# An attention scan with two gated layers on one core: the last two A parts in unit 13, the last substitution at 1.05 steps a part, weight conversions cut into single operations in units 18 to 23

## The chip, the cores and the metric

The kernel runs on one core of one Trainium2 chip. The metric is the device time of one execution in microseconds; the median of three runs of the kernel before is 929.41 us (926.57 to 936.09). The two halves of the kernel share one program: first the attention, whose last third holds the change, then two layers.

## The reference

Inputs are r, k, v, w, a, b of shape 4 x 8 x 768 x 40 (batch, head, step, head dim) in float32, and the weights of two layers. The layers' matrices w_in, w_out, w_in2, w_out2 and the taps are float64 and reach the chip as 64-bit words. The reference is, cut to its core:

```
for t in range(S):                       # S = 768, state: B x H x 40 x 40
    y[t]  = r[t] @ state
    Sa    = state @ a[t]
    state = state*w[t][None,:] - outer(Sa, b[t]) + outer(v[t], k[t])
x = y as (4, 768, 320)
h = relu(x @ w_in);  c = 3-tap convolution of h over steps
x = (h * sigmoid(c)) @ w_out
h = relu(x @ w_in2); u, v = halves of h
x = (u * (w_spatial @ normalized(v) + b_spatial)) @ w_out2
```

## The kernel before

**Units.** The scan is cut into 6 blocks of 128 steps (n = 0 to 5), each of two chunks of 64, for 4 batches (i = 0 to 3) with all 8 heads. A pair (i, n) is a unit; the 24 units are numbered kk = 4n + i. Two batches share a pair of tiles, so a block has two parts p = 2n + i//2. The state passes from unit kk to kk+4.

**The work of a unit** is written as four generators, each yielding after a few instructions. A(kk) (line 148) transposes AR and P on PE, lets ACT copy them to bdA (L159) and PT (L168), and multiplies them (L174); DVE masks the product into G (L175). The last A of a block sends a slice of G to DRAM (tb, L181, four DMAs). Bp(kk) (L231) applies the inverse triangular blocks DT and D1: pf, px, and pw, which ACT copies to WT (L296); POOL copies DT into bdN (L278). Cp(kk) (L317) is the step over the two chunks: pu on PE, its copy to ZU on ACT (L329), pm on PE, and on DVE pm and VM (L339, L341), from which the next chunk's pu is made. Units of the last block have no pm in their second chunk. Dp(kk) (L343) makes the output: pz and pv, ACT's copies ZV and bdR, pS, DVE's SS (L376), py and DVE's y (L387).

**The order.** In the main loop (line 483) each unit kk runs through a written string of 19 positions, `ORDER="CDCBDDCBDACAABBAADD"`. C steps Cp(kk), D steps Dp(kk-1), B steps Bp(kk+1), and A steps A(kk+LA) with LA = 9, nine units ahead. Unit 0 has two A parts, 8 and 9, interleaved in it, two steps at each letter A. Engines take their instructions in the order in which this loop emits them, and so do the DMA queues of SP. Each unit's own D part ends in the next unit. From unit 15 on there is no A part left, and the string's letters A do nothing.

**Ticks.** Every position is a tick. `later(m,f)` runs f after m ticks, in the order of the list. At every tick `pump` advances the background generators: `acc` grows by RATE0, RATE or RATE2 (1.25), and as many steps run as acc holds whole ones.

**Substitution** (subst, L185). When the fourth A part of a block has been emitted, subst(n) is started: LL ticks after (LL2 = 9 for the last) it loads L from tb (L189), SUB = 5 ticks after that it joins the background. For each j from 1 to 30 it does a product and a sum on DVE over (31-j) x j elements (L206, L208), one per step; then a copy LT (L211); DDL = 8 ticks after it, `put` stores LT and L to DRAM (dt, dd; L213, L214), and loadD (L219) loads them again as DT (L226) and D1 (L229), as soon as put has run and the B part before has been emitted. These are needed by the B parts of the block. L has one buffer.

**Weights.** Layer weights are converted from 64-bit words to float32 and split into a rounded part and its remainder, during the attention, by one generator (prep1, L618), 14 jobs after the taps: six of 128x512 (w_in), three of 128x320, four of 128x512 (two 256-wide blocks), one of eight 64-wide blocks. A job loads raw by SP (L595), one job ahead; ACT takes its absolute value into mo (L554), DVE does four operations (L555 to L558), and one step later ACT rounds (L606) and POOL subtracts (L607). In the attention the staging tiles use the buffers of tiles that are done with: raw those of AR (two), ct those of PT (two), mo that of bdA (one). The list EX gives the number of steps of this generator that are done by the end of units 14 to 23; within a unit they are spread evenly over the 19 positions. What is left runs with the last D part.

The loop's core, from line 485 on:

```
ahead=[... EARLY[kk] if kk<len(EARLY) else [kk+LA] if kk+LA<NK-2 or not LAST2
       else [NK-2,NK-1] if kk+LA==NK-2 else []]
...
for _ in range(max(1,len(ahead)) if g=='A' else 1): next(gens[g],None)
while done<ex(kk-1)+(ex(kk)-ex(kk-1))*(z+1)//19: next(later_layer,None); done+=1
tick(); acc+=RATE0 if kk<3 else RATE if kk<14 else RATE2; pump(int(acc)); acc-=int(acc)
```

Of the kernel before, what the change touches and what calls it, by code (L numbers as in the profile page):

```python
# [11 lines left out]
def attention(tc, keep, ident, vr,bk,w,a, x, spare=None):  # L12
    nc=tc.nc
# [3 lines left out]
    with ExitStack() as ctx:  # L17
# [69 lines left out]
        def later(m,f):  # L87
            due.append((now[0]+m,f)); 
        def tick():
            now[0]+=1  # L90
            for d in [d for d in due if d[0]<=now[0]]:
                due.remove(d); d[1]()
# [92 lines left out]
        def subst(n):  # L185
            if n not in Ls: Ls[n]=(sb.tile([128,HB*HB+HB],F32,name="L"),sb.tile([128,HB*HB//4],F32,name="tmp"),sb.tile([128,HB,HB],F32,name="LT"))
            flat,tmp,LT=Ls[n]
            L=flat[:,0:HB*HB].rearrange("p (t j) -> p t j",j=HB)
            BQ[0].dma_start(out=L,in_=tb_d[n])  # L189
            yield  # L190
            if n in SMALL:
                K=HB//2
                V.memset(L[:,K:,0:K],0.0)
                Q=flat.rearrange("p (s r) -> p s r",s=2)[:,:,0:K*HB].rearrange("p s (t j) -> p s t j",j=HB)[:,:,:,0:K]
                for j in range(1,K-1):
                    m=K-1-j
                    t=tmp[:,0:2*m*j].rearrange("p (s m k) -> p s m k",s=2,m=m)
                    V.tensor_tensor(t,Q[:,:,j+1:,j:j+1].to_broadcast([128,2,m,j]),Q[:,:,j:j+1,0:j].to_broadcast([128,2,m,j]),ALU.mult)
                    yield
                    V.tensor_tensor(Q[:,:,j+1:,0:j],Q[:,:,j+1:,0:j],t,ALU.add)  # L200
                    yield
            else:
                for j in range(1,HB-1):
                    m=HB-1-j
                    t=tmp[:,0:m*j].rearrange("p (m k) -> p m k",m=m)
                    V.tensor_tensor(t,L[:,j+1:HB,j:j+1].to_broadcast([128,m,j]),L[:,j:j+1,0:j].to_broadcast([128,m,j]),ALU.mult)  # L206
                    yield
                    V.tensor_tensor(L[:,j+1:HB,0:j],L[:,j+1:HB,0:j],t,ALU.add)  # L208
                    yield
            V.memset(flat[:,0:HB*HB:HB+1],1.0)  # L210
            V.tensor_copy(LT,L.rearrange("p t j -> p j t"))  # L211
            def put():
                BQ[0].dma_start(out=dt_d[n],in_=LT)  # L213
                BQ[0].dma_start(out=dd_d[n],in_=L if n in SMALL else L[0:128:2])  # L214
                stored.update((n,j) for j in range(2))
            later(DDL,put)
            yield
        inv={}; stored=set()
        def loadD(p):  # L219
# [175 lines left out]
        def pump(m):  # L395
            while m>0 and (bg or bg2):
                q=bg or bg2
                try: next(q[0])
                except StopIteration: q.pop(0); continue
                m-=1  # L400
# [10 lines left out]
        with tc.manual_schedule(engines={mybir.EngineType.SP,mybir.EngineType.DVE,mybir.EngineType.Activation}):  # L411
# [61 lines left out]
            with tc.manual_schedule():  # L473
                none=iter(()); acc=0.0; dg={}
                def staging(z):
                    def tmp():
                        mo=sb.tile([128,2,512],F32,name="mo",tag="bdA",bufs=1)
                        return [sb.tile([128,512],I32,name="ct",tag="PT",bufs=2),mo[:,0],mo[:,1]]
                    return (lambda: sb.tile([128,512,2],I32,name="raw",tag="AR",bufs=2)),tmp
                later_layer=spare(FC=512,staging=staging) if spare else none  # L480
                done=0
                ex=lambda kk: EX[kk-14] if kk>=14 else 0
                for kk in range(NK):
                    i,n=units[kk]
                    ahead=[z for z in (EARLY[kk] if kk<len(EARLY) else [kk+LA] if kk+LA<NK-2 or not LAST2 else [NK-2,NK-1] if kk+LA==NK-2 else []) if z<NK]
                    gens={'A':chain(*[A(z) for z in ahead]),'B':Bp(kk+1) if kk+1<NK else none,'C':Cp(kk),'D':dg.pop(kk-1) if kk else none}
                    gens['Z']=dg[kk]=Dp(kk)
                    if kk==6 or kk==14: lam_end(n+1)
                    po=(kk+LA)//2 if (kk+LA+1)%2 else (kk+LA+1)//2
                    z=-1  # L490
                    for g in ORDER if kk<TAIL else ORDER2:
                        if g=='W':
                            warm(ident,WM)
                            continue
                        z+=1
                        for _ in range(max(1,len(ahead)) if g=='A' else 1): next(gens[g],None)
                        if z in BX and kk+1<NK and units[kk+1][1] in SMALL: next(gens['B'],None)
                        while done<ex(kk-1)+(ex(kk)-ex(kk-1))*(z+1)//19:
                            next(later_layer,None); done+=1
                        tick(); acc+=RATE0 if kk<3 else RATE if kk<14 else RATE2; pump(int(acc)); acc-=int(acc)  # L500
                        for s,f in SCHED[(kk+LA+1)%2]+SCHEDC[kk%2]:
                            if s==z:
                                if f=='il' and kk==0: later(9,lambda po=po: l_il(po))
                                elif f=='dup' and kk==0: later(11,lambda po=po: l_dup(po))
                                elif f=='pm' and kk==1: later(4,lambda po=po: l_pm(po,V))
                                elif f=='Z' and kk==0: later(24-z,lambda kk=kk: loadZ(kk//2+1))
                                elif f=='Z': loadZ(kk//2+1)
                                elif f=='V': loadV(kk//2+1)
                                else: {'araw':l_araw,'ln':l_ln,'P':l_P,'g':l_g,'ar':l_ar,'il':l_il,'pm':(lambda p: l_pm(p,V)) if PMV else l_pm,'dup':l_dup}[f](po)
                    if any(z%4==3 for z in ahead): nxt=subst(ahead[-1]//4 if ahead[-1]%4==3 else ahead[0]//4); ll=LL if kk+LA<NK-2 else LL2; later(ll,lambda z=nxt: next(z)); later(ll+SUB,lambda z=nxt: bg.append(z))  # L510
                pump(1000)
                for _ in dg.pop(NK-1): next(later_layer,None)
                flush()

TAIL=24
LAST2=0
PUA=1
WM=2
ORDER2="DCCDDBCBACDADDABBAA"
# [1 line left out]
LA=9  # L521
L4T=14
RATE=1.25
RATE2=1.25
RATE0=1.4
SCHED=[[[1, "il"], [11, "araw"], [12, "ln"], [14, "g"], [15, "dup"], [16, "P"], [17, "ar"]], [[3, "pm"]]]
SCHEDC=[[[6, "Z"]], [[10, "V"]]]
SUB=5
TBL=3
LL2=9  # L530
LL=10
DDL=8
DTL=7
# [6 lines left out]
BX=(0,9)  # L540
DTLS=2
W=[34,9,9,12,12,9,8,8,10,10,6]
EX=[3, 7, 7, 9, 11, 15, 20, 24, 28, 30]

# [1 line left out]

def from_f64(nc,out,raw,tmp):

    t,m=tmp
    lw,up=raw[...,0],raw[...,1]
    V=nc.vector
    nc.scalar.activation(m,up.bitcast(F32),AF.Abs)  # L554
    V.tensor_scalar(out=t,in0=up,scalar1=3,scalar2=0x3fffffff,op0=ALU.logical_shift_left,op1=ALU.bitwise_and)  # L555
    V.scalar_tensor_tensor(out=t,in0=lw,scalar=29,in1=t,op0=ALU.logical_shift_right,op1=ALU.bitwise_or)
    V.scalar_tensor_tensor(out=t,in0=up,scalar=-0x40000000,in1=t,op0=ALU.bitwise_and,op1=ALU.bitwise_or)
    V.scalar_tensor_tensor(out=out,in0=m,scalar=TINY,in1=t.bitcast(F32),op0=ALU.is_ge,op1=ALU.mult)  # L558

def words(ap):  # L560
# [3 lines left out]
class Layers:  # L564
# [12 lines left out]
        return (lambda: L.vv([128,256,2],I32,z%3)), (lambda: [L.vv([128,256],d,3+z%2*3+q) for q,d in enumerate((I32,F32,F32))])  # L577


    def weight(L,w,places,FC=256,staging=None,low=None):  # L580


        nc=L.tc.nc; staging=staging or L.staging
        K,F=w.shape; n=-(-K//128); g=max(1,FC//F); fc=min(F,FC)
        jobs=[(k,min(g,n-k),f0) for k in range(0,n,g) for f0 in range(0,F,fc)]
        jobs=[(k,m,f0,min(fc,F-f0)) for k,m,f0 in jobs]
        stg={}
        def load(z):
            k0,m,f0,fc=jobs[z]
            raw,tmp=staging(z)  # L590
            raw=raw(); stg[z]=raw,tmp
            for q in range(m):
                k=k0+q; rows=min(128,K-k*128)
                for j in range(128//rows):
                    nc.sync.dma_start(out=raw[j*rows:(j+1)*rows,q*fc:(q+1)*fc],in_=words(w[k*128:k*128+rows,f0:f0+fc]))  # L595
        load(0)
        for z,(k0,m,f0,fc) in enumerate(jobs):
            if z+1<len(jobs): load(z+1)
            yield
            fs=slice(f0,f0+fc); raw,tmp=stg.pop(z)  # L600
            t,a,o=[x[:,:m*fc] for x in tmp()]
            from_f64(nc,o,raw[:,:m*fc],(t,a))
            yield
            for q in range(m):
                h,l=places(k0+q); oq=o[:,q*fc:(q+1)*fc]
                nc.scalar.copy(h[:,fs],oq)  # L606
                (low or nc.gpsimd).tensor_tensor(l[:,fs],oq,h[:,fs].bitcast(F32),ALU.subtract)  # L607
                if K%128 and k0+q==n-1: nc.gpsimd.memset(l[64:128,fs].bitcast(F32),0.0)
# [467 lines left out]
```

## Time and profile before

| | |
|---|---|
| median of 3 runs | 929.41 us (926.57 to 936.09) |
| profiled execution | 931.44 us, span 929.7 us |
| granted TensorE clock, mean | 0.946 |
| PE busy | 851.0 us, 92% |
| PEld busy | 792.9 us, 85% |
| DVE busy | 650.9 us, 70% |
| ACT busy | 524.3 us, 56% |
| POOL busy | 225.4 us, 24% |

PE is TensorE's matmuls, PEld its weight loads, DVE VectorE, ACT ScalarE, POOL GpSimd, SP SyncE, which issues the DMAs. A row of the timeline has the start (us from the span's start), the duration, the engine, the line of the kernel, the operation, output and input tile, the count of instructions merged into the row, and in brackets the idle time of the engine before it with what ended it. A row of groups has the summed busy time, the mean duration in ns, and the idle time before. A granted clock of 1.00 stands for 2.4 GHz and 0.50 for 1.2 GHz; a window's figure is the mean over it. Matmul ends are modelled.

### The profile page before, as it was taken

How to read it: one execution, taken by the hardware profiler on the slowest of the kernel's cores; microseconds unless marked ns; L12 is line 12 of the kernel's file. 1: busy time of each engine (PE TensorE's matmuls, PEld its weight loads, DVE VectorE, ACT ScalarE, POOL GpSimd, SP SyncE). 2: the span in 40 equal slices, each digit the busy share in tenths (PEclk: the TensorE clock that was granted, in tenths of full speed). 3: DMA queues.
4: the chain of work that ended last, by engine and by line, in shares of the span. 5: the costliest groups of instructions: out<-in, count | busy, mean ns of one | idle time of the engine just before them, and what ended most of it. 6: DMA issues, size and time to landing. Idle time of an engine off the chain costs nothing. (4 is left out here: it accounts for less than half of the span.)

```text
span 929.7 us, 23445 instructions
## 1 busy us (share of the span) xinstructions
PE 851.0 (92%) x9575; PEld 792.9 (85%) x9575; DVE 650.9 (70%) x1472; ACT 524.3 (56%) x1157; POOL 225.4 (24%) x308
## 2 busy tenths in 40 slices
PE   0888689999999999899988889999999999999997
PEld 0577579999989898788976779999999999999997
DVE  6877795596794878976569978357674667656673
ACT  0463575777767766668655655267433764267421
POOL 2110110222221313224310011245221541235221
PEclk9975697999999999989789899999999999999999
DMA  8989894745648436235221330110021001110011
GB/s 215 218 199 211 155 214 92 162 111 134 141 99 195 85 90 171 68 110 152 81 81 56 98 100 8 47 48 1 1 86 40 23 1 47 55 43 1 1 32 57
DMA packets 149189, 86.70 MB, mean 93 GB/s; under 512 B 124176, under 2 KB 138256, under 8 KB 147152
## 3 DMA queue, kind: packets, MB, share of 16 engines
q1 hardware_dynamic: 148800, 84.78, 37.4%
q8 instruction: 77, 1.26, 0.6%
q14 instruction: 40, 0.33, 0.1%
q10 hardware_dynamic: 272, 0.33, 0.1%
HBM read 61.24 MB, written 23.86 MB: 92 GB/s over the span
## 5 line engine op out<-in xcount | busy, mean ns | idle before, releaser
L697 PE MATMUL psp<-spt,vv 128*128 128x384 f32 x576 | 105.5, 338 | 0.5 <-DVE vv L825 0.3
L697 PE MATMUL ph<-XT,G 128*128 128x386 f32 x512 | 101.5, 344 | 0.7 <-DVE XT L730 0.7
L697 PEld LDWEIGHTS psp<-spt,vv 128*128 128x128 f32 x576 | 100.2, 188 | 2.1 <-ACT vv L822 1.0
L697 PEld LDWEIGHTS ph<-XT,G 128*128 128x128 f32 x512 | 92.6, 191 | 1.1 <-DVE XT L730 1.0
L759 POOL TENSOR_TENSOR gl<-c,gh 128x384 fp32r<-128x384 f32 x48 | 66.2, 1379 | 72.1 <-ACT gh L757 57.6
L773 PE MATMUL acc<-gh,G 128*128 128x384 f32 x320 | 68.6, 343 | 9.4 <-ACT gh L757 7.0
L331 POOL COPY ZU<-ZU 64x320 f32<-64x320 f32 x48 | 26.2, 546 | 193.2 <-ACT ZU L329 187.3
L755 DVE TENSOR_TENSOR c<-h,c 128x384 f32<-128x384 f32 x64 | 39.9, 623 | 44.0 <-ACT c L752 43.8
L773 PEld LDWEIGHTS acc<-gh,G 128*128 128x128 f32 x320 | 56.8, 191 | 13.9 <-ACT gh L757 9.7
L174 PE MATMUL p<-PT,bdA 80*128 80x128 f32 x384 | 57.1, 311 | 6.1 <-ACT PT L168 6.1
L208 DVE TENSOR_TENSOR L<-L,tmp 128x30 f32<-128x30 f32 (+9 forms) x150 | 58.7, 391 | 4.1
L174 PEld LDWEIGHTS p<-PT,bdA 80*128 80x128 f32 x384 | 53.4, 223 | 9.3 <-ACT PT L168 9.2
L206 DVE TENSOR_TENSOR tmp<-L 128x30 f32<-128x30 f32 (+9 forms) x150 | 52.6, 350 | 9.7 <-DMA L<-tb 5.9
L375 PE MATMUL pS<-bdR,ZV 80*128 80x128 f32 x384 | 57.1, 294 | 2.0 <-DVE ZV L369 1.5
L846 ACT CAST zh<-u 128x384 fp32r<-128x384 f32 x28 | 14.4, 514 | 73.6 <-DVE u L843 73.6
L847 POOL TENSOR_TENSOR zl<-u,zh 128x384 fp32r<-128x384 f32 x28 | 31.6, 1128 | 98.6 <-ACT zh L846 87.3
L329 ACT COPY ZU<-pu 64x160 f32<-64x160 f32 x96 | 27.5, 286 | 49.6 <-PE pu L327 47.8
L375 PEld LDWEIGHTS pS<-bdR,ZV 80*128 80x128 f32 x384 | 49.3, 201 | 3.7 <-DVE ZV L369 1.7
L295 PE MATMUL pw<-bdN,G 128*104 128x128 f32 x384 | 50.7, 290 | 0.9 <-issue 0.9
L175 DVE TENSOR_TENSOR G<-p,mT 128x512 f32<-128x512 f32 x48 | 32.8, 688 | 25.2 <-PE p L174 24.8
L757 ACT CAST gh<-c 128x384 fp32r<-128x384 f32 x64 | 32.9, 514 | 30.8 <-DVE c L755 28.3
L842 DVE TENSOR_TENSOR psp<-psp,bb 128x384 f32<-128x384 f32 x32 | 18.1, 566 | 45.4 <-PE psp L697 45.2
(186 smaller groups left out, 2118.3 us busy)
## 6 DMA issues: line engine op xcount, KB each, us to landing
P<-in_bk_dram SPq DMA_DIRECT2D x12, 640.0 KB, 5.1
ZU<-in_vr_dram SPq DMA_DIRECT2D x12, 640.0 KB, 7.3
lq<-in_w_dram SPq DMA_DIRECT2D x12, 320.0 KB, 6.8
araw<-in_a_dram SPq DMA_DIRECT2D x12, 320.0 KB, 6.3
lam<-lq SPq DMA_DIRECT2D x12, 320.0 KB, 4.4
lnA<-lam SPq DMA_DIRECT2D x12, 320.0 KB, 7.0
ilam<-lq SPq DMA_DIRECT2D x12, 320.0 KB, 5.5
il<-ilam SPq DMA_DIRECT2D x24, 160.0 KB, 4.3
```

Of the source, the lines that this page charges most:

```text
L174: T.matmul(p3[:,j],lhsT=bdA[:,g*4+j].rearrange("p c t -> p (c t)"),rhs=PTs[g][:,j],start=True,stop=True)
L175: V.tensor_tensor(G[:,hs,0:2*C],p3,mT.rearrange("p a t -> p (a t)").unsqueeze(1).to_broadcast([128,4,2*C]),ALU.mult)
L206: V.tensor_tensor(t,L[:,j+1:HB,j:j+1].to_broadcast([128,m,j]),L[:,j:j+1,0:j].to_broadcast([128,m,j]),ALU.mult)
L208: V.tensor_tensor(L[:,j+1:HB,0:j],L[:,j+1:HB,0:j],t,ALU.add)
L295: T.matmul(p[:104,j],lhsT=G[:,h0+g*4+j,C:],rhs=N[:,g*4+j],start=True,stop=True)
L375: T.matmul(p[:,j].rearrange("p c t -> p (c t)"),lhsT=ZV[:,j,0:2*C],rhs=bdR[:,j].rearrange("p c t -> p (c t)"),start=True,stop=True)
L697: L.tc.nc.tensor.matmul(out,lhsT=l,rhs=r,start=start and i==0,stop=stop and i==len(prs)-1)
L755: V.tensor_tensor(c,h[:,1:TH+1],c,ALU.mult)
L757: AC.copy(gh,c)
L759: def low(v): v.tensor_tensor(gl,c,gh.bitcast(F32),ALU.subtract)
L773: nc.tensor.matmul(acc[m],lhsT=l,rhs=r,start=f==0 and z<5 and z in (0,1,3),stop=f==NF-1 and z>=5)
L847: nc.gpsimd.tensor_tensor(gl,u,gh.bitcast(F32),ALU.subtract)
```

## The change

The last two A parts, 22 and 23, run together in unit 13, two steps at each letter A, as parts 8 and 9 do in unit 0; unit 14 has none. The last substitution is started from unit 13: its load 17 ticks after that unit, its background steps 5 later. RATE2 is 1.05 steps a tick, and it holds from unit 15 on. The last block's put comes 4 ticks after its LT, not 8. A conversion job's four DVE operations are steps of their own, with one empty step behind them, so a job has six steps and not two; the new list EX puts them in units 18 to 23, after the taps in unit 14. mo uses the buffer of bdA and that of il in turn.

```diff
--- before.py
+++ after.py
@@ -213,7 +213,7 @@
                 BQ[0].dma_start(out=dt_d[n],in_=LT)
                 BQ[0].dma_start(out=dd_d[n],in_=L if n in SMALL else L[0:128:2])
                 stored.update((n,j) for j in range(2))
-            later(DDL,put)
+            later(DDL if n<NU-1 else 4,put)
             yield
         inv={}; stored=set()
         def loadD(p):
@@ -474,10 +474,10 @@
                 none=iter(()); acc=0.0; dg={}
                 def staging(z):
                     def tmp():
-                        mo=sb.tile([128,2,512],F32,name="mo",tag="bdA",bufs=1)
+                        mo=sb.tile([128,2,512],F32,name="mo",tag=("bdA","il")[z%2],bufs=1)
                         return [sb.tile([128,512],I32,name="ct",tag="PT",bufs=2),mo[:,0],mo[:,1]]
                     return (lambda: sb.tile([128,512,2],I32,name="raw",tag="AR",bufs=2)),tmp
-                later_layer=spare(FC=512,staging=staging) if spare else none
+                later_layer=spare(FC=512,staging=staging,fine=True) if spare else none
                 done=0
                 ex=lambda kk: EX[kk-14] if kk>=14 else 0
                 for kk in range(NK):
@@ -497,7 +497,7 @@
                         if z in BX and kk+1<NK and units[kk+1][1] in SMALL: next(gens['B'],None)
                         while done<ex(kk-1)+(ex(kk)-ex(kk-1))*(z+1)//19:
                             next(later_layer,None); done+=1
-                        tick(); acc+=RATE0 if kk<3 else RATE if kk<14 else RATE2; pump(int(acc)); acc-=int(acc)
+                        tick(); acc+=RATE0 if kk<3 else RATE if kk<15 else RATE2; pump(int(acc)); acc-=int(acc)
                         for s,f in SCHED[(kk+LA+1)%2]+SCHEDC[kk%2]:
                             if s==z:
                                 if f=='il' and kk==0: later(9,lambda po=po: l_il(po))
@@ -513,7 +513,7 @@
                 flush()
 
 TAIL=24
-LAST2=0
+LAST2=1
 PUA=1
 WM=2
 ORDER2="DCCDDBCBACDADDABBAA"
@@ -521,13 +521,13 @@
 LA=9
 L4T=14
 RATE=1.25
-RATE2=1.25
+RATE2=1.05
 RATE0=1.4
 SCHED=[[[1, "il"], [11, "araw"], [12, "ln"], [14, "g"], [15, "dup"], [16, "P"], [17, "ar"]], [[3, "pm"]]]
 SCHEDC=[[[6, "Z"]], [[10, "V"]]]
 SUB=5
 TBL=3
-LL2=9
+LL2=17
 LL=10
 DDL=8
 DTL=7
@@ -540,21 +540,28 @@
 BX=(0,9)
 DTLS=2
 W=[34,9,9,12,12,9,8,8,10,10,6]
-EX=[3, 7, 7, 9, 11, 15, 20, 24, 28, 30]
+EX=[3, 3, 3, 3, 17, 31, 46, 60, 80, 88]
 
 
 
 TINY=3.4332275390625e-05
 
 def from_f64(nc,out,raw,tmp):
+
+    for _ in f64_steps(nc,out,raw,tmp): pass
+
+def f64_steps(nc,out,raw,tmp):
 
     t,m=tmp
     lw,up=raw[...,0],raw[...,1]
     V=nc.vector
     nc.scalar.activation(m,up.bitcast(F32),AF.Abs)
     V.tensor_scalar(out=t,in0=up,scalar1=3,scalar2=0x3fffffff,op0=ALU.logical_shift_left,op1=ALU.bitwise_and)
+    yield
     V.scalar_tensor_tensor(out=t,in0=lw,scalar=29,in1=t,op0=ALU.logical_shift_right,op1=ALU.bitwise_or)
+    yield
     V.scalar_tensor_tensor(out=t,in0=up,scalar=-0x40000000,in1=t,op0=ALU.bitwise_and,op1=ALU.bitwise_or)
+    yield
     V.scalar_tensor_tensor(out=out,in0=m,scalar=TINY,in1=t.bitcast(F32),op0=ALU.is_ge,op1=ALU.mult)
 
 def words(ap):
@@ -577,7 +584,7 @@
         return (lambda: L.vv([128,256,2],I32,z%3)), (lambda: [L.vv([128,256],d,3+z%2*3+q) for q,d in enumerate((I32,F32,F32))])
 
 
-    def weight(L,w,places,FC=256,staging=None,low=None):
+    def weight(L,w,places,FC=256,staging=None,low=None,fine=False):
 
 
         nc=L.tc.nc; staging=staging or L.staging
@@ -599,7 +606,10 @@
             yield
             fs=slice(f0,f0+fc); raw,tmp=stg.pop(z)
             t,a,o=[x[:,:m*fc] for x in tmp()]
-            from_f64(nc,o,raw[:,:m*fc],(t,a))
+            if fine:
+                yield from f64_steps(nc,o,raw[:,:m*fc],(t,a))
+                yield
+            else: from_f64(nc,o,raw[:,:m*fc],(t,a))
             yield
             for q in range(m):
                 h,l=places(k0+q); oq=o[:,q*fc:(q+1)*fc]
```

## Rows read from the trace of the kernel before

**Rows 1.** Windows of one unit each (15 to 20, 22, last D): busy us (count), clock, DMA.

```profile
347.80:359.70 11.90, 11.76 (x246) 10.84 (x244) 7.81 (x15) 9.87 (x23) 3.69 (x7) 1.00 0.71 209
359.70:374.90 15.20, 13.44 (x249) 12.28 (x246) 14.19 (x34) 7.23 (x19) 3.68 (x7) 0.89 0.55 106
374.90:387.00 12.10, 11.54 (x245) 10.69 (x243) 11.35 (x26) 8.81 (x21) 2.82 (x6) 1.00 0.09 31
387.00:405.70 18.70, 14.48 (x250) 13.38 (x246) 14.88 (x34) 8.46 (x21) 4.46 (x8) 0.82 0.55 141
405.70:417.20 11.50, 11.50 (x246) 10.70 (x244) 8.53 (x15) 9.84 (x23) 5.08 (x9) 1.00 0.29 86
417.20:428.10 10.90, 10.87 (x233) 10.07 (x230) 7.67 (x14) 8.99 (x23) 5.37 (x9) 1.00 0.70 159
...
439.20:456.00 16.80, 15.62 (x232) 14.55 (x230) 8.41 (x13) 9.52 (x26) 6.74 (x12) 0.70 0.20 64
464.20:473.30 9.10, 7.19 (x100) 6.51 (x96) 5.80 (x11) 2.96 (x13) 2.41 (x10) 0.86 0.62 197
```

**Rows 2.** Timeline of PE, rows of units 16 to 18, 22, last D part.

```profile
366.48 0.67 PE L327 MATMUL pu<-VM,WT 104*64 104x40 f32 x16 [1.09 <-DVE VM L341]
...
380.17 0.66 PE L327 MATMUL pu<-VM,WT 104*64 104x40 f32 x16 [0.56 <-DVE VM L341]
...
396.04 1.08 PE L327 MATMUL pu<-VM,WT 104*64 104x40 f32 x16 [3.84 <-DVE VM L341]
...
441.88 1.04 PE L338 MATMUL pm<-ZU,P 128*40 128x40 f32 x16 [1.13 <-ACT ZU L329]
...
469.06 1.16 PE L375 MATMUL pS<-bdR,ZV 80*128 80x128 f32 x8 [1.48 <-DVE ZV L369]
```

**Rows 3.** Groups of DVE instructions by line and shape, units 15 to 22 (347.8 to 456).

```profile
L376 DVE TENSOR_TENSOR SS<-pS,mS 128x512 f32<-128x512 f32 x16 | 10.9, 690 | 11.6 <-PE pS L375 11.5
...
L339 DVE TENSOR_TENSOR pm<-pm,VM 40x320 f32<-40x320 f32 x13 | 6.6, 509 | 5.1 <-PE pm L338 4.8
...
L557 DVE SCALAR_TENSOR_TENSOR ct<-raw,ct 128x512 int32<-128x512 int32 x9 | 6.2, 692 | 0.3
L555 DVE TENSOR_SCALAR ct<-raw 128x512 int32<-128x512 int32 x9 | 3.9, 438 | 0.1
...
L211 DVE COPY LT<-L 128x1024 f32<-128x1024 f32 x1 | 1.0, 1040 | 0.0
```

**Rows 4.** Groups by line and shape, whole span: one of the widest substitution steps.

```profile
L208 DVE TENSOR_TENSOR L<-L,tmp 128x238 f32<-128x238 f32 x10 | 4.1, 407 | 0.3
```

**Rows 5.** Timeline of ACT around the starts of units 20 and 22.

```profile
417.51 0.62 ACT L606 CAST G<-mo 128x512 fp32r<-128x512 f32 x1 [0.76 <-DVE mo L558]
...
440.99 0.67 ACT L554 ACTIVATE mo<-raw 128x512 f32<-128x512 f32 x1 [1.40 <-POOL G L607]
```

**Rows 6.** Timeline of ACT and of PE in the A part of unit 13.

```profile
325.14 1.26 ACT L159 ACTIVATE bdA<-p,mB 80x512 f32<-80x512 f32 x2 [0.91 <-PE p L157]
326.42 1.35 ACT L315 COPY VM<-ZU 64x640 f32<-64x640 f32 x2
327.67 1.05 ACT L168 COPY PT<-p 80x512 f32<-80x512 f32 x2
...
325.70 1.07 PE L167 MATMUL p<-ident,P 128*80 128x128 f32 x8
...
328.36 1.99 PE L174 MATMUL p<-PT,bdA 80*128 80x128 f32 x16
```

**Rows 7.** DMA issues in 385 to 395, with the time to landing.

```profile
ZU<-in_vr_dram SPq DMA_DIRECT2D x1, 640.0 KB, 7.0
```

**Rows 8.** Timelines of POOL and of DVE around 361.8.

```profile
361.73 1.31 POOL L607 TENSOR_TENSOR G<-mo,G 128x512 fp32r<-128x512 f32 x1 [4.75 <-ACT G L606]
...
361.66 0.25 DVE L206 TENSOR_TENSOR tmp<-L 128x84 f32<-128x84 f32 x1
361.94 1.20 DVE L208 TENSOR_TENSOR L<-L,tmp 128x84 f32<-128x84 f32 x1
```

## The prediction

> **What bounds the kernel now.** I read the page's table of busy time first: PE 92%, the others far below, so the end moves only where PE waits or runs at its lower clock. Then the stretch the diff touches, units 13 to 23, was cut into windows of one unit each, from one unit's last py matmul to the next one's. They show an undisturbed pace without an A part: 11.5 us in unit 19 and 10.9 in unit 20, whose last batch has one pm less [rows 1]. Units 15 to 22 together took 108.2 us (347.8 to 456.0); at 11.5 for 15 to 19 and 10.9 for 20 to 22 they would take 90.2. The 18.0 us between sit in three units: 16 (3.7 too long), 18 (7.2) and 22 (5.9); the others share 1.2.
>
> PE's timeline says what they are [rows 2]: PE idles 1.09 and 3.84 us in units 16 and 18 before pu of chunk 1, which waits for DVE's VM (L341), and 1.13 us in unit 22 before pm, which waits for ACT's ZU copy. Behind each the granted clock falls, from 2.4 to 1.2 GHz for a time: 0.89, 0.82 and 0.70 in those windows. (1 - clock) times the window is 1.7, 3.4 and 5.0 us, which with the idle nearly makes each excess. Behind the idle of 0.56 in unit 17 the window shows 1.00. So a wait of about 1.1 us has twice cost more than itself, and one of half that has not.
>
> Why DVE is late: a unit's own DVE work is two SS at 0.69, two pm at 0.51, two VM and one y at about the same: 3.9 us [rows 3]. The substitution adds 23.75 steps a unit; the widest are 0.41 [rows 4], so 9.7, and a whole conversion adds 0.44 + 3 x 0.7 = 2.6 [rows 3]. Units 16 and 17 ask for 3.9 + 9.7 = 13.6, more in 17 with its conversion, of a PE unit of 11.5. Unit 18 pays. Why ACT is late in unit 22: its abs (L554) waits 1.40 us for POOL's subtraction, because there is one tile mo, and ZU stands behind it [rows 5].
>
> **The change part by part.** *A parts.* PE, ACT and DVE issue the same instructions one unit earlier; the count is the same. New is that steps run in pairs. From the end of A's first transposes ACT owes bdA 1.26, VM 1.35 and PT 1.05, 3.7 us, before the second half of L174 can run; PE has in between the P transposes (1.07), pm (0.8 at full clock, 1.04 in [rows 2]) and half of L174 (1.0), 2.9 [rows 6]. Before, pw's 1.9 us stood there too. So PE waits about 0.8, and I add 0.6 for the second part, whose PT copies follow two WT copies: 1.4. Bounds: 0, if ACT is early, and 3.7. Against it, unit 13's DVE gains 3.7 us of PE time for 1.4 us of work, so it ends less late, for which I credit 0.4. Net +1.0. The tb stores go to SP 19 positions earlier, and the load of L follows at unit 14's position 16, behind the last but one part's dt and dd stores; L is there before unit 15's position 2, since DVE has little to do in unit 14.
>
> *Substitution.* It starts at unit 15's position 2 and not 13, at 20 steps a unit, and ends at unit 18's position 2 (before 4). DVE from VM to VM: units 15 to 16 about 20 narrower steps, between 0.25 [rows 8] and 0.41 [rows 4], 20 x 0.33 = 6.6, + 3.9 = 10.5; 16 to 17 the widest, 20 x 0.43 with gaps, 8.6 + 3.9 = 12.5; 17 to 18 as the first. PE's pu stands about 5 us into a unit and pm's result is there at 2.4; VM is done 1.0 later, so DVE may be some 1.4 late. 12.5 is under 11.5 + 1.4: I take 0.3 (0 to 0.6). The excess of units 15 to 18 goes.
>
> *Conversions.* Three jobs of 2.6 leave units 15 to 17; all 14 now stand in units 18 to 23. DVE in unit 18 then has LT 1.04 [rows 3], 2.33 conversions (6.1), 0.4 of steps and 3.9: 11.4. Units 19 to 21 have 10 or less, unit 22 three conversions, 7.8 + 2.9 (no second pm): 10.7 of 11. The second tile costs nothing, as il's last reader is unit 13's pm; it takes away the wait of 1.40, and with it unit 22's 5.9. What is late next is ACT's queue. At the end of unit 18 DVE can't finish a conversion before about 11.8 us into the unit: pm of chunk 1 arrives at 8, the steps come behind it (unit 19's did so: the split waited 0.76, ended 0.9 us into unit 20, and PE didn't wait for the ZU behind it [rows 5]). Now the abs of the next conversion, 0.67, stands between split and ZU, and PE waits 0.6. That abs also needs raw 2, whose load is issued only when conversion 0 has read its tile, some 7 us into unit 18, and on SP behind the put, moved by the shorter delay from position 12 to 6, and so ahead of the ZU load: 0.5 + 0.25 + 0.64 MB stand before it. A ZU load took 7.0 us to land [rows 7]; with 4 to 8 us for raw 2 it lands 11 to 15 us into unit 18, where 12.4 is wanted. So PE waits 0.6 to 3.2 in unit 19; I take 1.7, the middle, and, being over 1.1, the 3.4 of clock of unit 18: 5.1 (0.6 to 8). The other places where a split or abs now precedes ZV or bdN in units 20 to 22 I price at 1.3 together (0 to 2.5), for ACT is filled to nearly 11 us in unit 22. POOL's subtraction beside DVE steps adds 0.6, less than one case of it in [rows 8].
>
> *End.* Conversion 13, 2.6 us of DVE, left the last unit's D part: its pS waited 1.48 [rows 2] and the clock was 0.86 over 9.1 us, 1.3 more [rows 1]. -2.8 (0 to -3.5).
>
> **Sum.** -18.0 - 2.8 + 1.0 + 0.3 + 5.1 + 1.3 + 0.6 = -12.5 us. The profiled execution took 931.44, 2.0 above the median of 929.41; so 918.9 by it and 917 as a median. Behind this stretch PE is busy to the end, and nothing there waits for a fixed time.
>
> **Rivals.** *Unit 19 stays covered.* raw 2 lands in time and no wait reaches 1.1 us: 0.6 in place of 5.1, and POOL costs nothing: -17.6, 912. For it: loads of this kind mostly land while SP waits; against: the order on SP.
>
> *The clock falls twice more.* The doubled A part's 1.4 us and unit 22's ACT queue each cost 3.4 of clock and 0.2 of idle besides: -5.3, 924. For it: 1.09 was enough in unit 16. Against: the 1.4 lies in three pieces.
>
> *POOL blocks DVE.* A 128x84 step took 1.20 us while POOL's subtraction ran, its neighbour of the same size 0.25 [rows 8]: 0.95 lost. If each conversion met one so, unit 18 would need 11.4 + 2.2 = 13.6, unit 19 12, unit 22 13.5 of 11: some 2.8 us of PE waits and one fall of 3.4, less the 0.6 taken: -6.9, 923. Against: most subtractions of before stood beside DVE instructions that weren't slowed, and their number is unchanged. The Trainium skill's page "SBUF — State Buffer", section "SBUF: two separate sides", says that GpSimd and a DVE instruction with two SBUF inputs lock each other out of one port pair for the whole instruction; by that rule every step and two of four conversion operations are exposed, and the sum would be this rival's. The trace agrees for the step at 361.94.
>
> *Slower: ACT's queue.* Splits spread over all positions wait for DVE, ZU stands behind each, and as in unit 22 before a wait of 1.13 costs 5.9 in all. If units 19 to 22 and 13 all pay this, 29 us, and the end gains nothing: -18.0 + 29 + 0.3 = +11.3, 941. It decides where a split meets ZU with DVE over 1 us late. Against: ACT's sum fits in every unit, and before, splits at the same place waited only 0.76.
>
> **Numbers.** Forecast 0.40, unit 19 covered 0.24, two clock falls 0.14, POOL 0.10, slower 0.12. The forecast's own range is 911 to 922. From 909 (the second case with the A part and ACT's places at zero) to 928 (the third with its bounds up) about 0.2 is left out. A measurement of this kernel tells some 1%, 9.3 us, from no change. Faster by more: 0.24 and two thirds of 0.40, 0.52; within: 0.36; slower: 0.12.
>
> **What would show it.** Right: windows of units 15 to 18 near 11.5 with clock 1.00, no L554 waiting for POOL, pS at the end without 1.48. Unit 19's first pm shows the wait for ZU, and ACT's abs that for raw. Wrong: VM waits above 1 us in units 17 or 18, a lower clock in unit 13 or 14, or several units of 18 to 22 with ACT behind DVE.

## The result and the profile after

The kernel after takes 939.36 us (median of 12 runs, 934.11 to 956.51) against 930.25 us (12 runs, 926.57 to 939.32) before: a ratio of 1.0098, 95% interval [1.007, 1.0126]. It is about 1% slower, where 917 us and a range up to 928 were forecast. A ratio compares undisturbed executions alone, so it can differ a little from the quotient of two medians.

The profiled execution took 944.82 us, span 943.0. Of the 13.3 us by which its span is longer than that of before, 4.8 had come about before unit 13, where both kernels run the same code, and 0.6 after the last D part; 7.96 belong to the stretch of the change, from the end of unit 12 to the end of the last D part (156.06 us before, 164.02 after). It is cut here into one window a unit, as in [rows 1]; the columns are the window and its length, PE busy, the granted clock, the DMA share and GB/s.

```profile
322.00:342.40 20.40, 19.14 (x306) 1.00 0.15 34
342.40:354.32 11.92, 11.92 (x248) 1.00 0.67 142
354.32:373.04 18.72, 16.18 (x247) 0.73 0.63 160
373.04:384.59 11.55, 11.55 (x248) 1.00 0.23 37
384.59:396.15 11.56, 11.56 (x247) 1.00 0.09 33
396.15:407.69 11.54, 11.54 (x247) 1.00 0.46 132
407.69:428.37 20.68, 16.92 (x248) 0.67 0.55 140
428.37:440.52 12.15, 10.95 (x231) 1.00 0.66 138
440.52:451.51 10.99, 10.85 (x231) 1.00 0.41 133
451.51:464.95 13.44, 12.67 (x232) 0.87 0.31 98
464.95:478.20 13.25, 9.37 (x146) 0.79 0.63 179
478.20:486.02 7.82, 7.82 (x98) 0.70 0.17 63
```

The rows are units 13 to 23 and the last D part. Units 16, 17 and 18 stand at exactly the pace that was forecast, 11.5 us at a clock of 1.00, where [rows 1] has 15.2, 12.1 and 18.7. Against that stand unit 15 (18.7), unit 19 (20.7) and unit 23 (13.3). PE's timeline names the wait in each; [rows 2] has another list altogether:

```profile
358.99 0.69 PE L272 MATMUL pf<-DT,G 32*32 32x32 f32 x32 [2.54 <-DMA DT<-dt]
...
412.85 1.47 PE L338 MATMUL pm<-ZU,P 128*40 128x40 f32 x16 [3.76 <-ACT ZU L329]
...
474.56 0.44 PE L383 MATMUL py<-P,SS 128*64 128x40 f32 x4 [3.75 <-DVE SS L376]
```

The first wait is for a load. The other two name ACT and DVE, but each of these had waited for a load itself. ACT's timeline in unit 19 (the abs, and ZU's copy right behind it), then DVE's in units 19 and 23 (the first operation of a conversion, and SS behind it):

```profile
411.94 0.68 ACT L558 ACTIVATE mo<-raw 128x512 f32<-128x512 f32 x1 [3.31 <-DMA raw<-in_moe_w_in_dram]
412.53 0.58 ACT L329 COPY ZU<-pu 64x160 f32<-64x160 f32 x2
```

```profile
411.89 0.43 DVE L559 TENSOR_SCALAR ct<-raw 128x512 int32<-128x512 int32 x1 [3.90 <-DMA raw<-in_moe_w_in_dram]
...
473.35 0.43 DVE L559 TENSOR_SCALAR ct<-raw 128x512 int32<-128x512 int32 x1 [5.20 <-DMA raw<-in_moe_w_out_dram]
473.81 0.69 DVE L376 TENSOR_TENSOR SS<-pS,mS 128x512 f32<-128x512 f32 x1
```

SP's timeline shows how the three loads came to be late (start of the issue, time of the issue or issues):

```profile
341.16 3.13 SPq L181 DMA_DIRECT2D tb<-G  x4
344.34 1.87 SPq L624 DMA_DIRECT2D traw<-in_moe_conv_w_dram  x3
346.31 0.54 SPq L310 DMA_DIRECT2D ZU<-in_vr_dram  x1
349.28 0.34 SPq L213 DMA_DIRECT2D dt<-LT  x1
...
354.63 0.37 SPq L226 DMA_DIRECT2D DT<-dt  x1
...
402.82 0.66 SPq L310 DMA_DIRECT2D ZU<-in_vr_dram  x1
403.59 0.53 SPq L602 DMA_DIRECT2D raw<-in_moe_w_in_dram  x1
...
466.28 0.40 SPq L389 DMA_DIRECT2D x<-lnA  x1
466.80 4.96 SPq L602 DMA_DIRECT2D raw<-in_moe_w_out_dram  x8
```

In unit 13, SP stood in front of the tb stores until the last A part was done (341.16), and the taps and ZU went out behind them, then dt, dd and DT. DT's load was issued at 354.63, when unit 15 had begun: unit 14 is 3.7 us shorter than before, so PE reached pf before DT was there. L's load stands behind DT and D on SP, and it was late as well, as DVE's timeline shows: the first step of the substitution, planned for unit 15's position 2, ran 6.3 us into the unit.

```profile
360.60 0.24 DVE L206 TENSOR_TENSOR tmp<-L 128x30 f32<-128x30 f32 x1 [3.08 <-DMA L<-tb]
```

Raw 2 went out at 403.59, behind dt, dd and ZU, and landed 8.3 us later. Raw 13's eight loads followed the store of unit 21's y.

### The profile page after: what moved, and what is told of

It reads as the page before. It is cut to its first block, busy times and chain, and to the rows that moved or that the text cites. A ratio compares the mean times of both kernels' runs of the same rounds, so it can differ in the third digit from the quotient of the medians.

```text
span 943.0 us, 23435 instructions
## 1 busy us (share of the span) xinstructions
PE 861.0 (91%) x9575; PEld 801.6 (85%) x9575; DVE 649.7 (69%) x1472; ACT 524.2 (56%) x1157; POOL 230.7 (24%) x308
## 3 DMA queue, kind: packets, MB, share of 16 engines
q8 instruction: 77, 1.26, 0.6%
## 5 line engine op out<-in xcount | busy, mean ns | idle before, releaser
L375 PE MATMUL pS<-bdR,ZV 80*128 80x128 f32 x384 | 60.0, 305 | 1.1 <-ACT ZV L369 0.8
L206 DVE TENSOR_TENSOR tmp<-L 128x30 f32<-128x30 f32 (+9 forms) x150 | 52.2, 348 | 12.1 <-DMA L<-tb 8.2
L208 DVE TENSOR_TENSOR L<-L,tmp 128x30 f32<-128x30 f32 (+9 forms) x150 | 55.6, 371 | 4.0
L295 PE MATMUL pw<-bdN,G 128*104 128x128 f32 x384 | 54.0, 301 | 2.1 <-POOL bdN L278 0.9
L375 PEld LDWEIGHTS pS<-bdR,ZV 80*128 80x128 f32 x384 | 52.5, 212 | 2.5 <-ACT ZV L369 1.3
L295 PEld LDWEIGHTS pw<-bdN,G 128*104 128x104 f32 x384 | 50.2, 193 | 3.5 <-POOL bdN L278 1.6
L121 POOL TENSOR_TENSOR G<-araw,lnA 128x640 f32<-128x640 f32 x12 | 19.5, 1622 | 131.5 <-DMA tb<-G 48.9
```

What stands on the lines that cost most here:

```text
L295: T.matmul(p[:104,j],lhsT=G[:,h0+g*4+j,C:],rhs=N[:,g*4+j],start=True,stop=True)
L375: T.matmul(p[:,j].rearrange("p c t -> p (c t)"),lhsT=ZV[:,j,0:2*C],rhs=bdR[:,j].rearrange("p c t -> p (c t)"),start=True,stop=True)
```

## The experiments

The theory at the start: the pacing does what it was meant to, and the whole loss lies in three loads that lost their place on SP or the time that had covered them, each charged twice, as a wait and as a lower clock behind it. The rivals: the paired A parts themselves, or DVE and ACT filled with single operations. The first four kernels take one load each, then all.

**The tb stores later.** `later(TBL,put)` becomes `later(TBL if n<NU-1 else 11,put)`.

> One edit to the kernel after: the last block's tb stores leave 11 positions after their A part and not 3, so that on SP they stand behind the taps and the ZU load. Theory (covers lost): in unit 15 of the kernel after PE's pf waits 2.54 us for the load of DT and then runs 10.24 us at half clock, because SP waits with the tb stores in its front until A(23) has ended and issues ZU, dt, dd and DT's load behind them. With the stores behind, ZU's load goes out some 20 us earlier, DT's load about 3 us earlier; unit 15's window goes from 18.7 to 11.5 to 13 us and its clock to 1.00, the whole kernel loses 5.5 to 7.5 us (about 932 to 934). Units 19 and 23 keep their waits of 3.8 us each. Rival 1 (the doubled A part itself sets unit 15's time, through DVE's or ACT's lateness): unit 15 stays at 18 to 19 us, the time within 1.5 us of the kernel after. Rival 2 (the chain LT, dt, DT is late by itself, unit 14 being 3.7 us shorter): pf still waits 1.5 to 2.5 us and unit 15 gains under 1.5 us.

Measured: 938.74 us, ratio to before 1.0073 [1.0036, 1.011]. Unit 15's window is

```profile
347.23:358.77 11.54, 11.54 (x247) 1.00 0.90 239
```

ZU's load goes out 8.0 us behind unit 12's end (322.85 less 314.90) where it was 24.3 (346.31 less 322.00), and pf has no wait. DT's load goes out 2.8 us behind dt's store (342.19 to 344.97), and 5.4 us behind it in the kernel after (349.28 to 354.63). So unit 15's loss was the order on SP, and neither the paired A parts nor a chain late by itself.

The medians differ from the kernel after by 0.6 us only, less than the 5.5 to 7.5 expected. Two things in the profiles bear on it. Kernels that leave the tb stores alone show pf's wait at 2.00 to 2.69 us, but not always the lower clock (last section), so that the edit is worth 2 to 7 us from one execution to the next. And in this profile units 16, 17, 19 and 20 are together 4.6 us longer than in the kernel after. In units 16 and 17 (12.38 and 12.61 us, clock 1.00) PE waits 0.76 and 0.99 for VM, in PE's timeline of unit 17

```profile
376.73 0.66 PE L327 MATMUL pu<-VM,WT 104*64 104x40 f32 x16 [0.99 <-DVE VM L341]
```

because here too the substitution can't start before 6.0 us into unit 15, where DVE has waited 2.74 for L. The kernel after has no VM wait in these units: its 18.7 us in unit 15 gave DVE the time to catch up. How much of the missing gain each of the two accounts for isn't shown.

**put later.** `later(DDL if n<NU-1 else 4,put)` becomes `later(DDL,put)` again.

> One edit to the kernel after: the last block's put stands 8 positions after LT again and not 4, so that on SP the load of raw 2 goes out ahead of the dt and dd stores and the ZU load. Theory: in unit 19 of the kernel after, ACT's abs waits 3.31 us for raw 2, ZU's copy stands behind it, PE's pm waits 3.76 us for ZU and then runs 13.65 us at half clock. With raw 2 ahead it lands some 3 to 4 us earlier, pm's wait falls under 0.6 us, unit 19's window goes from 20.7 to 11.5 to 12.1 us, the whole kernel loses 7.5 to 9 us (about 930 to 932), less 0 to 1.2 us if DT's load for unit 20 is now late. Rival 1 (DVE has too much work in units 18 and 19 with conversions as single operations, the load being late only beside it): raw's wait goes, but ZU waits for the split in its place, over 1.5 us, and the window stays above 16 us. Rival 2 (the transfer itself is slow, 8 us from its issue, whatever stands before it on SP): abs still waits 2 us or more.

Measured: 939.77 us, 1.0122 [1.0058, 1.0185]. Raw 2's wait has gone, and nothing is won: PE waits for DT in its place. SP's timeline, then PE's:

```profile
395.38 0.36 SPq L602 DMA_DIRECT2D raw<-in_moe_w_in_dram  x1
395.79 0.42 SPq L213 DMA_DIRECT2D dt<-LT  x1
...
403.79 0.37 SPq L226 DMA_DIRECT2D DT<-dt  x1
```

```profile
402.38 1.04 PE L338 MATMUL pm<-ZU,P 128*40 128x40 f32 x16 [0.38 <-ACT ZU L329]
...
407.44 1.06 PE L272 MATMUL pf<-DT,G 32*32 32x32 f32 x32 [4.01 <-DMA DT<-dt]
```

Behind raw 2's 0.5 MB, DT's load could start only 8.0 us after the dt store was issued; before, with nothing in front, 2.8 us (397.85 to 400.65). The theory's mechanism holds, its remedy doesn't: both loads want the queue within 2 us of each other, and the theory had put the second one at 1.2 us at most. The Trainium skill, page "DMA: Bandwidth & Descriptors", section "Queues, rings and completion order", says that each DMA engine takes descriptors in ring order. These rows fit that: dt's store took 7.9 us from issue to landing with raw 2 ahead of it, and 2.7 in the kernel before. They don't tell standing in line from sharing the engines.

**Job 13 as one load.** For a job of eight pieces the eight `dma_start` become one, with both sides rearranged to (p, q, f, two).

> One edit to the kernel after: the eight small loads of job 13 (w_out's last 64 columns) are one load of the same bytes. Theory: in unit 23 of the kernel after PE's py waits 3.75 us for SS on DVE, which stands behind a conversion operation that waits 5.20 us for raw 13, whose eight loads SP issued from 466.8 to 471.8 us, after the store of unit 21's y. As one load all of it is issued about 4.5 us earlier and lands 3 to 4.5 us earlier: py waits 0 to 1 us, unit 23's window goes from 13.3 to 9 to 10.5 us, the whole kernel loses 2.5 to 4.5 us. Rival 1 (the store ahead of it on SP, not the eight issues, makes it late): under 1 us of the wait goes. Rival 2 (small rows of 512 B make one load as slow as eight): it lands no earlier than 1.5 us before, py still waits 2 us or more.

Measured: 946.95 us, 1.019 [1.0136, 1.0243]. py's wait shrinks from 3.75 to 3.34 us: SP's timeline, then DVE's:

```profile
457.21 0.39 SPq L389 DMA_DIRECT2D x<-lnA  x1
457.73 1.54 SPq L600 DMA_DIRECT2D raw<-in_moe_w_out_dram  x1
```

```profile
463.41 0.43 DVE L559 TENSOR_SCALAR ct<-raw 128x512 int32<-128x512 int32 x1 [4.42 <-DMA raw<-in_moe_w_out_dram]
```

The one load takes 5.7 us from issue to use, the eight took 6.5 from the first issue. Rival 1 is borne out: DVE finishes unit 21's y at 457.19, the store that waits for it goes out at 457.21, and the load only behind that. Rival 2's sign is met as well, since the one load is only 0.9 us quicker: neither form comes in time from this place. That the median is 7.6 us above the kernel after was not foreseen; the profile (937.32 us) doesn't show it, and it stays open.

**All three.**

> The three edits together: tb stores 11 positions after A, put 8 positions after LT, job 13 as one load; the A parts in unit 13, 1.05 steps a position and the single operations stay as in the kernel after. Theory (three loads that lost their place or cover hold all of the loss): the gains add, 16 to 20 us less than the kernel after, 920 to 924 us, 0.6 to 1.1% less than the kernel before; no PE wait above 1.1 us from unit 14 to 23. Rival (each wait removed uncovers the next, since ACT and DVE are full with conversions in units 18 to 23): less than 10 us of it comes, 930 or more, with new waits of 1 us and more for ZU, ZV or bdN in units 20 to 23.

Measured: 937.58 us, 1.0073 [1.0035, 1.0112]. The rival is right on the time, but its cause, ACT and DVE full with conversions, isn't shown: unit 15 is at 11.54, unit 19 at 22.41 with a wait of 4.36 for DT, and py waits 2.79; these waits are for loads again. In units 20 to 22 bdN waits 1.06 and ZV 0.59, about what the kernel after has. Moving loads one at a time isn't enough.

The next four separate the halves of the change.

**Whole conversions.** The kernel after with the later tb stores, the old list EX, `fine` off, and one tile mo; then the same with two tiles.

> The A parts in unit 13 and the last substitution at 1.05 steps a position, with the tb stores 11 positions after their A part, and the conversions as in the kernel before: whole ones at their old places, two steps a job, one tile mo. Theory now: the A parts and the substitution do what they were forecast to do, and the loss comes with the conversions' new places (raw 2 and DT want the queue at the same time in units 18 and 19; raw 13 in unit 23). So units 18 to 20 show 11.5, 11.6 and 10.9 us, unit 22 keeps the 16.8 of the kernel before (ZU behind an abs that waits for mo), the last D part its pS wait of about 1.5; units 15 to 17, which hold three whole conversions, 11.5 to 13.5 each. Sum from unit 13 on 146 to 150 us where the kernel before has 156.0: 921 to 925 us. Rival (the shorter units 16 to 18 themselves uncover the chain LT, dt, DT, whatever the conversions do): pf in unit 19 waits 2 us or more here as well, and the time is 928 or more.

> As as_coarse, with the second tile for mo. Theory: L554's waits for POOL's subtraction go, with them ZU's wait in unit 22, whose window falls from 16.8 to 11 to 12.5 us; 4 to 6 us less than as_coarse, 916 to 920 us, 1.2 to 1.6% under the kernel before. Rival (unit 22's wait is ACT's queue and not the tile): unit 22 stays above 15 us, the time within 1.5 us of as_coarse.

Measured: 941.23 us, 1.0075 [1.0034, 1.0115], and 936.19 us, 1.0049 [1.0009, 1.0089]. On unit 19 the theory is right: 11.55 us, no wait for DT with one tile, 1.43 us of wait with two. On the tile it is right as well: unit 22 falls from 16.77 to 11.21. But the sum is missed, since units 15 to 18, which still hold four whole conversions, aren't smooth. Window of unit 16, and ACT's timeline in it, with one tile:

```profile
370.01:387.18 17.17, 13.25 (x247) 0.90 0.49 94
```

```profile
374.42 0.62 ACT L616 CAST G<-mo 128x512 fp32r<-128x512 f32 x1 [5.12 <-DVE mo L565]
```

DVE is 5 us late with a conversion, the split stands in front of ZU, and PE waits 3.88. So this half alone is no gain: the even substitution needs units 15 to 17 free of conversions.

**Conversions alone**, on the kernel before.

> The conversions' part of the change alone on the kernel before: single operations in units 18 to 23 and two tiles; A parts in units 13 and 14, 1.25 steps a position, put 8 positions after LT as before. Theory: unit 16 loses its fall (15.2 to 11.6 us), unit 18 comes down from 18.7 to 12 to 15 us since three conversions left DVE, unit 22 from 16.8 to 12 to 13.4; but raw 2 now stands ahead of dt and dd on SP, and pf in unit 19 waits 2 to 4.5 us for DT (unit 19 at 14 to 22 us), and unit 23's py waits 3 to 4 us for SS behind raw 13 (unit 23 at 13 to 14 us). Sum near that of the kernel before: 924 to 933 us. Rival (the single operations do no harm by their places; the harm comes from the earlier put and the shorter units): units 19 and 23 show no wait over 1 us, the time is 915 to 920 us.

Measured: medians of 935.79 and 932.57 us, ratio 0.9979 [0.9932, 1.0027], no difference. The median is above the 924 to 933 expected. The profiled execution, of 942.39 us, shows the waits expected: unit 19's pm waits 1.68 for ZU and pf 2.22 for DT, unit 23's py 3.51 for SS, while units 16 and 22 are at 11.55 and 13.25. Unit 17 has one that wasn't expected, 1.26 for VM (14.57 us). The loads of units 19 and 23 are the conversions' own doing, with or without the A parts.

**Another order on SP.** The later tb stores; in unit 18 `later(8,...)` in front of loadZ; EX ends in 82, 83, so that raw 13 is loaded in unit 22.

> The kernel after with its loads in another order on SP and nothing else: tb stores 11 positions after A, the ZU load of unit 18 8 positions later (so that SP issues dt, dd, raw 2, DT, D, ZU where it issued dt, dd, ZU, raw 2, DT, D), and job 13's load at the end of unit 22, ahead of unit 21's store, with its operations in the last D part. Theory (order on SP): raw 2 lands 3 to 4 us earlier, DT at most 1 us later than in the kernel after; unit 15 11.5 us, unit 19 11.5 to 13 us, unit 23 8.2 to 9.5 us, last D part 8 to 9.5 us: 11 to 17 us less than the kernel after, 921 to 927 us. Rival (the bytes wanted in units 18 and 19 are too many whatever their order: dt, dd, raw 2, DT, D, ZU, raw 3): pm or pf in unit 19 still waits 2 us or more, and the gain is only that of units 15 and 23, 3 to 9 us.

Measured: 932.5 us, 0.9994 [0.9959, 1.0029], 7 us less than the kernel after by the medians: level with before, short of the 921 to 927. In unit 19 PE still waits 2.45 for ZU. SP's timeline and DVE's say why:

```profile
389.27 0.64 SPq L603 DMA_DIRECT2D raw<-in_moe_w_in_dram  x1
```

```profile
388.16 0.69 DVE L564 SCALAR_TENSOR_TENSOR ct<-raw,ct 128x512 int32<-128x512 int32 x1
...
397.01 0.43 DVE L560 TENSOR_SCALAR ct<-raw 128x512 int32<-128x512 int32 x1 [2.58 <-DMA raw<-in_moe_w_in_dram]
```

No order can bring raw 2 earlier: its tile is free at 388.85, when job 0's L564 has read it, the load goes out 0.4 us later, and DVE has it 7.7 us behind that. It is DVE that comes too soon, one job later. Unit 23 (17.04) has a new wait: pu for WT, 1.52, behind the conversions crowded into unit 22.

**No loads at all, new places for the operations, and work in the wait.**

```
no_loads:  if cnt>=2: stg[z]=kept[cnt%2],tmp; return   # in load(z)
spread:    order_fix, EX=[3, 3, 3, 3, 15, 27, 45, 63, 81, 82]
warm19:    if kk==19 and z==1: warm(ident,24)
```

> The kernel after with the tb stores 11 positions after A, in which the conversions from job 2 on read the two tiles that hold jobs 0 and 1 again: their loads are left out (the weights are then wrong), every operation on ACT, DVE and POOL stands where it stood. Theory (the loads, not the operations, hold the loss): units 15 to 18 at 11.5 to 12.4 us, unit 19 at 11.5 to 12.3 without a wait for raw or DT, unit 23 at 8.2 to 9 and the last D part near 7.8; unit 20's wait for bdN (1 us) and unit 22's for ZV (0.6) may stay, for they stand behind operations. Sum from unit 13 on 139 to 145 us where the kernel before has 156.0 and the kernel after 164.0: 914 to 921 us, 1.2 to 1.9% under the kernel before. Rival (single operations spread over the positions put ACT's copies behind DVE, loads or not): ZU waits of 1 us and more stay in units 19 to 23, time 925 or more.

> order_fix with the steps of the conversions placed anew: 12 in unit 18, 12 in unit 19, 18 in each of units 20 to 22, the rest in the last two stretches (order_fix had 14, 14, 15, 14, 22), so that job 2's first operation stands 3 positions later and unit 22 has one conversion less. Theory: in order_fix raw 2 was issued right behind the operation that freed its tile, at 389.3 us, and landed 7.6 us later, and DVE wanted it 2.6 us before that; with 1.8 us more, the wait is under 1 us and stands behind ZU: unit 19 at 11.5 to 13 us (20.2 there), unit 23 at 8.2 to 10 us (17.0 there, where pu waited for WT behind three operations). 8 to 14 us less than order_fix in these units: 919 to 925 us, 0.8 to 1.4% under the kernel before. Rival (three conversions in a unit are too many for ACT and DVE wherever they stand): units 20 to 22 show waits over 1 us for ZU, bdN or VM and windows over 13 us, the time is 928 or more.

> The kernel after with 24 matmuls of ident by ident put at the second position of unit 19, ahead of the pm that waits 3.76 us for ZU: PE works where it waited. Theory (the wait costs twice, itself and the lower clock behind it): pm's wait shrinks to under 1 us, the clock stays at 2.4 GHz through the unit, and unit 19 takes 15 to 16.5 us in place of 20.7, of which 11.5 are its own work. Rival (the half clock comes from somewhere else, or the wait is all): the unit stays at 19 us or more, with a clock under 0.8.

Measured: no_loads 924.38 us against 935.13 for before on that chip, 0.9882 [0.9826, 0.9937]; **spread 922.92 us, 0.9872 [0.983, 0.9914]**, 1.3% under the kernel before; warm19 938.69 us, one run. The windows of units 19 to 22 of spread:

```profile
399.92:412.03 12.11, 11.81 (x248) 1.00 0.74 187
412.03:423.20 11.17, 10.84 (x224) 1.00 0.64 158
423.20:435.56 12.36, 11.52 (x232) 1.00 0.69 169
435.56:448.33 12.77, 11.18 (x226) 1.00 0.32 105
```

Unit 19 has no wait over 0.3 us, and all four clocks are 1.00. With fewer steps in units 18 and 19, job 2's abs stands behind ZU's copy, so a late load no longer holds up PE; ACT's timeline:

```profile
401.23 0.60 ACT L329 COPY ZU<-pu 64x160 f32<-64x160 f32 x2
...
403.23 0.69 ACT L559 ACTIVATE mo<-raw 128x512 f32<-128x512 f32 x1
```

The stretch from unit 12's end to that of the last D part is 145.8 us, 10.3 less than before; with the loads left out it is 148.5. So the single operations as such aren't the loss: where they stand, without the loads and with the tb stores later, the kernel is 1.2% under the kernel before, and no ZU wait is above 0.4 us. The loss lies in when the loads arrive against the operations that need them. The last piece, unit 23 and its D part, is 18.4 in spread (17.2 before): no gain there, though unit 23 was expected at 8.2 to 10 us and took 11.3. no_loads was expected at 914 to 921 us; in it unit 19 was to have no wait for DT, but pf waits 0.98 us for it, and the unit takes 17.82, as PE's timeline and the window show:

```profile
405.35 0.69 PE L272 MATMUL pf<-DT,G 32*32 32x32 f32 x32 [0.98 <-DMA DT<-dt]
```

```profile
401.58:419.40 17.82, 16.45 (x249) 0.71 0.41 78
```

warm19 prices the clock. Unit 19, and PE's timeline in it:

```profile
405.98:422.91 16.93, 16.93 (x296) 1.00 0.62 156
```

```profile
407.21 5.54 PE L410 MATMUL warm<-ident 128*128 128x128 f32 x48
412.69 0.81 PE L338 MATMUL pm<-ZU,P 128*40 128x40 f32 x16
```

Each of the 24 calls leaves two records. ZU is just as late (its copy starts 4.5 us into the unit, 4.8 in the kernel after), but PE works where it waited, for 5.5 us, longer than the wait; the clock stays at 2.4 GHz, and the unit takes 3.75 us less than the 20.68 of the kernel after, where 4.2 to 5.7 less were expected. Of the kernel after's 9.1 us too many, 3.76 were the wait; the other 5.4 went with the lower clock, as its PE was busy 16.92 us with what takes 11.55 at a clock of 1.00. This is one profile of each; one execution, 938.69 us, can't tell 4 us from none.

**The new list of steps alone** on the kernel after.

> The kernel after with only the new list of conversion steps of spread (12, 12, 18, 18, 18, then 1 and the rest); tb stores and the ZU load of unit 18 where the kernel after has them. Theory: unit 15 keeps its wait for DT of 2.0 to 2.7 us (window 13.6 to 18.7 us), since tb stands ahead of taps and ZU; units 19 and 23 gain most of what spread gained: in unit 19 the abs of job 2 now stands behind ZU's copy, so pm has no wait over 0.6 us and DVE alone waits up to 2 us for raw 2 (unit 19 at 11.5 to 14 us); unit 23 and the last D part together 16 to 19 us (21.1 in the kernel after). 926 to 932 us, 0.3 to 1.0% under the kernel before. Rival (it was the order on SP that mattered in unit 19): ZU or VM still waits over 1.5 us behind raw 2, unit 19 at 16 us or more, the time 933 or more against a kernel before of 931.

Measured: 932.13 us, 1.0032 [0.9993, 1.007]. The mechanism is nearly as the theory has it: unit 15 still shows the wait for DT, and in unit 19 DVE waits 1.80 for raw 2 and PE only 0.25 for ZU. A wait of 1.40 for DT in its place wasn't expected:

```profile
346.82:365.39 18.57, 16.20 (x249) 0.72 0.64 161
...
400.04:413.61 13.57, 11.88 (x247) 1.00 0.63 159
```

The time isn't under the kernel before, where 0.3 to 1.0% under it was expected. Of the ratios to before, 1.0098 is that of the kernel after, 1.0032 with the new places alone, 0.9994 with the order on SP alone (order_fix), 0.9872 with both: both are needed for the 1.3%.

## Why the prediction was wrong

By its own steps, against the profiled stretch (+7.96 us where -12.5 was forecast). The 20.5 us between are unit 15 (7.2), the end (6.7), unit 19 (4.0), units 20 to 22 (2.0) and the A parts (0.6). Two steps failed by their mechanism, unit 15 and the end: both go by the engines' work, where the arrival of a load decided.

*Units 16 to 18: right, with some luck.* 11.55, 11.56 and 11.54 us; 11.3 us gained. No VM wait of 1 us, as the price of 12.5 us of DVE in unit 17 said. But unit 15's stall helped: with the tb stores later, units 16 and 17 show VM waits of 0.76 and 0.99, in spread one of 0.36 in unit 17, where 0.3 was the price. The A parts cost 1.6 over units 13 and 14, where I had 1.0.

*Unit 15: failed, 7.2 us.* The step is "L is there before unit 15's position 2, since DVE has little to do in unit 14". L wasn't there: DVE waited for it until 6.3 us into the unit, and in every later kernel that starts the substitution here until 4.5 us or more. The step followed L behind the tb stores and the dt and dd of the last but one part, but not all that stands behind the tb stores on SP: taps, ZU, dt, dd and DT. It also credited unit 14 with its 3.7 us without asking which load that time had covered. The wait of 2.54 and the clock took 6.8 us; the step had no term for it, and 0.4 of gain.

*Unit 19: the mechanism was right, its size wrong, +9.1 for +5.1.* Place, chain and cause stand as forecast (abs waits for raw 2, ZU behind it, PE's pm). The 1.7 us was the middle of 0.6 to 3.2; it is 3.76, because raw 2 took 8.3 us to land behind ZU, above the 8 that I had as an end. The clock's 3.4 us, taken from unit 18 before, are 5.4.

*Units 20 to 22: half right, -2.2 for -4.2.* The second tile took away unit 22's wait for ZU, but 0.94 for bdN in unit 20 and 0.59 for ZV in unit 22, with a clock of 0.87, took some of it back.

*End: failed, +3.9 for -2.8.* pS's wait of 1.48 went, as forecast. But the step took the conversion to be only DVE's work moved from one stretch to another. Job 13 is a weight of its own, whose load isn't sent one job ahead; its place was two positions ahead of its use, behind a store. In the kernel before the load went out at the same store (457.20), but its first operation ran at 464.72, 7.5 us later; in the kernel after DVE stood ready for it 1.4 us behind the issue.

*The rivals.* "ACT's queue" gave 941, near the result by luck: ZU did stand behind an abs, but that was to come from DVE's lateness in units 19 to 22, and it came from loads. "The clock falls twice more" put the falls in unit 13, which kept 1.00, and in unit 22, where one cost 1.8 us of PE time; its price of 3.4 is under the 4.6 and 5.4 of units 15 and 19. "POOL blocks DVE" did happen without deciding anything: in the kernel after an L563 took 1.66 us beside POOL's subtraction, and 0.69 elsewhere, but PE's waits in units 15, 19 and 23 were for loads. It counts two of a conversion's four operations as having two inputs; by the kernel's lines they are three, all but the first, and even a first one (L559, at 431.64) took 1.52 beside a subtraction, against 0.43.

The forecast of what an even pace is worth came near: spread has the even pace and the loads in place, and in its one profile the stretch is 10.3 us shorter, of 12.5 forecast.

## What to carry to other kernels

A stall that is taken away had been covering something: for each unit that gets shorter, list the loads that land in it and whose issue is fixed by position, and ask each for its margin. When a step moves on a queue, follow everything behind it there, not only what depends on it. And where a late operand can't come sooner because its buffer is only then free, move its consumer, and keep short copies that PE needs ahead of it on the engine.

## What the runs showed of the hardware

Whether the clock falls behind a wait isn't told by the wait's length. In unit 15, at the same place, waits of 2.54, 2.37 and 2.29 us (the kernel after, steps_only, warm19) came with a granted clock of 0.73, 0.72 and 0.72 over the unit, but waits of 2.69 and 2.00 (put later, one load) with 1.00 and windows of 14.3 and 13.6 us. Up to there the five kernels run the same code. Put later's window:

```profile
351.23:365.54 14.31, 11.62 (x248) 1.00 0.81 209
```

In no_loads a wait of 0.98 us came with 0.71, with the tb stores later one of 0.99 with 1.00. So one wait costs 2 or 7 us, and single profiles differ by that much: the verdicts above go by the ratios, the places by the profiles. The Trainium skill, page "TensorE: Matmul & The Clock Gate", section "What's actually happening", states that the moment at which the clock changes depends on when the work falls, and so varies from run to run. It says so of the rise; that the fall varies as well is what these rows show.
